# The final store split over two queues, and the instruction streams emitted into a Block, in a one-core decode kernel

## The chip, the cores and the metric

The kernel runs on one core of a Trainium2 chip. A core has five engines with instruction streams of their own: TensorE (PE, with its weight loads shown as PEld), VectorE (DVE), ScalarE (ACT), GpSimd (POOL) and SyncE (SP), and 16 DMA engines that carry the transfers which SP and ACT issue here. The engines are kept in step by semaphores alone. The metric is the device time of one execution in microseconds (us); less is better.

## The reference

One token is decoded. With `xn`, the normalised input, the output is `x + A(xn) + B(xn)`: A is attention with grouped heads over a long cache, B a small block that mixes shifted channels and then applies a two-layer MLP.

```python
# A: 32 query heads, 4 key/value heads, cache of 65536 positions, head size 128, D = 1024
q = (xn_A @ wq).reshape(1, 1, 32, 128).transpose(0, 2, 1, 3)
scores = einsum("bhqd,bhkd->bhqk", q, repeat(k_cache, 8, axis=1)) * 128 ** -0.5
o = einsum("bhqk,bhkd->bhqd", softmax(scores), repeat(v_cache, 8, axis=1))
A = o.transpose(0, 2, 1, 3).reshape(1, 1, 4096) @ wo
# B: F = 3584
h = gelu(layernorm(xn) @ w1)
x1 = xn + concat(shifted quarters of h) @ w2
B = x1 + gelu(layernorm(x1) @ w3) @ w4
return x + A + B          # 1 x 1 x 1024, bfloat16
```

The K and V caches are 67 MB each; with the weights, 170 MB are read from memory, and 2 KB are written.

## The kernel before

**Tiles.** K and V come in pairs of sub-tiles: a transfer of 4 MB brings 16384 positions of one head into one of two slots of `Kn` or `Vn`. Each sub-tile of 8192 positions (`NT` = 32 of them) goes through the same steps: VectorE transposes it (`Ttr`, line 463), TensorE multiplies with the queries (`QK`, line 475), VectorE and TensorE find a bound of the maximum (lines 482 to 492), ScalarE takes exponentials (`EXP`, line 505), TensorE and VectorE turn the result (lines 514 and 516), TensorE multiplies with V (`PV`, line 523), and ScalarE and GpSimd fold it into a running sum (`FLASH`, lines 531 to 537). The weights of B and of the output projection are loaded and used between sub-tiles, at places listed in `w_seq`. The last of them, w4, comes in four parts into the K slots (`w4_parts`), the smallest part last.

**Queues.** The order of each engine's work is written out by hand. An object of the class `_Q` (line 14) collects, for each engine, a list of waits, operations and transfers; `_op`, `_grp` and `_dma` (line 116) add to it, and work out from the buffers' last readers and writers which semaphores must be waited for. Only at the end does `emit` (line 43) go through a list and produce the engine's instructions. A wait that an instruction can't carry itself becomes a semaphore instruction with the line number 46. All loads are issued by SP, in the order of the list, but for the input `x` (2 KB), which ACT issues as its first instruction (line 275). The first loads are the two halves of wq (line 272), then K and V of the first pair (line 286).

**The opening.** What is built ahead of the kernel's function (line 640) fills a few constants on POOL and ends with a barrier over all five engines: four of them drain and count up one semaphore, POOL drains, waits for the four, and counts up a second semaphore, for which the four wait. After the barrier each engine's stream goes on with its own first instruction, without a jump.

**The end.** The output is summed in PSUM over all stages in four rows of 256 columns, on partitions 0, 32, 64 and 96 (`out_rows`, line 391). After the last part of w4 VectorE casts them into `orow` (line 618), SP issues one transfer of four rows of 512 bytes (line 619) and waits until it has landed. Then SP's stream is over; the other engines' streams end with their own last operation.

Of the kernel before, what the change touches and what calls it, by code (L numbers as in the profile page):

```python
# [72 lines left out]
def _deps(q, reads, writes):  # L73
    for b in reads:
        for s, v in b.w.items():
            q.wait((s, v))
    for b in writes:
        for s, v in b.w.items():
            q.wait((s, v))
        for s, v in b.r.items():  # L80
            q.wait((s, v))


def _done(ev, reads, writes, partial=False):
    for b in reads:
        b.add_read(ev)
    for b in writes:
        if partial:
            b.add_write(ev)
        else:  # L90
            b.set_write(ev)


def _op(q, fn, reads=(), writes=(), partial=False):
    _deps(q, reads, writes)
    ev = q.op(fn, True)
    _done(ev, reads, writes, partial)
    return ev
# [17 lines left out]
def _dma(q, chan, fn, reads=(), writes=(), partial=False):  # L116
    _deps(q, reads, writes)
    chan.n += 1
    ev = q.dma(fn, chan.sem, 16 * chan.n)
    _done(ev, reads, writes, partial)  # L120
    return ev


def bass_parallel_sum__gqa_block_cached__mixer_s_mlp__decode_kernel(
# [29 lines left out]

    with ExitStack() as es:
        E = es.enter_context

        def sb(name, shape, dt):
            return E(nc.sbuf_tensor(name, shape, dt))

        def ps(name, shape, dt):
            return E(nc.psum_tensor(name, shape, dt))

        def sem(name):
            return E(nc.semaphore(name))

# [51 lines left out]
        orow = sb("orow", [P, 256], BF)  # L218
# [15 lines left out]
        q_pe = _Q("pe", sem("c_pe"))  # L234
        q_dve = _Q("dve", sem("c_dve"))
        q_act = _Q("act", sem("c_act"))
        q_pool = _Q("pool", sem("c_pool"))
        q_sp = _Q("sp", None)
        chans = {}

        def chan(name):
            if name not in chans:
                chans[name] = _DmaChan(sem("d_" + name))
            return chans[name]
# [83 lines left out]
        def layer_norm(src, b_src, dst_f, dst_bf, b_dst, c0):  # L328
# [29 lines left out]
            reads=[b_M1, b_misc], writes=[b_misc])  # L358
# [19 lines left out]
        for h in range(HKV):  # L378
            for we in range(4):
# [3 lines left out]
                    reads=[b_M1, b_const], writes=[b_Y], partial=(h + we > 0))  # L383
# [232 lines left out]
        for i in range(len(w4_parts)):  # L616
            w4_pe(i)
        _op(q_dve, lambda e: e.tensor_copy(orow[:, :], OUT_ps[:, 0:256]), reads=[b_OUT], writes=[b_orow])
        ev_out = _dma(q_sp, chan("out"), lambda e: e.dma_start(out=out[0, 0, :].rearrange("(j n) -> j n", j=4), in_=orow[0:97:32, :]), reads=[b_orow])
        q_sp.wait(ev_out)  # L620

        q_sp.emit(nc.sync)
        q_act.emit(nc.scalar)
        q_pool.emit(nc.gpsimd)
        q_dve.emit(nc.vector)
        q_pe.emit(nc.tensor)


# [26 lines left out]
```

## Time and profile before

| | us |
|---|---|
| median of 3 runs (402.83 to 402.92) | 402.84 |
| the profiled execution | 402.83 |
| its span, first to last instruction | 401.6 |

| engine | busy us | share of the span |
|---|---|---|
| DVE | 227.8 | 57% |
| PE | 187.7 | 47% |
| POOL | 62.0 | 15% |
| ACT | 48.4 | 12% |

The DMA engines read 169.87 MB, 423 GB/s over the span. The profile is taken on one execution; the span runs from the first instruction of the program to the last, and the time of the execution is 1.23 us longer. In the views that follow, a line L272 is line 272 of the kernel before; SPq or POOLq is the sequencer of that engine, which issues transfers, waits and drains; an arrow `<-` in brackets names what ended the idle time ahead of a group. The chain of work that ended last is 54% DMA, 24% DVE and 17% PE.

### The profile page before, as it was taken

Reading aid. Unit: us, or ns where it says so; the run is one execution under the profiler, and the core shown is the slowest. Engines: PE = TensorE matmul, PEld = TensorE weight load, DVE = VectorE, ACT = ScalarE, POOL = GpSimd, SP = SyncE. Lnnn points to the kernel's source line nnn. Section 1 sums busy time; section 2 is a strip of 40 time slices with the busy share of each in tenths; the row PEclk is TensorE's granted clock in tenths of the full one; section 3 lists DMA queues with packets and bytes.
Section 4 is the critical chain, followed back from the end, with each engine's and each line's share of the span. In section 5 each row is a group of like instructions: output and inputs, shape, how many; then the busy total and the mean of one; then the engine's idle time right before and its main releaser. Section 6 shows DMA issues by size and latency. Waiting matters only on the chain.

```text
span 401.6 us, 5142 instructions
## 1 busy us (share of the span) xinstructions
PE 187.7 (47%) x2043; PEld 84.2 (21%) x2059; DVE 227.8 (57%) x400; ACT 48.4 (12%) x127; POOL 62.0 (15%) x90
## 2 busy tenths in 40 slices
PE   0361445064525745275630966353433545344674
PEld 0250111021103511062110731121111311111142
DVE  0217666277806588255753387676836775778410
ACT  0000211011101011011110011111201111112100
POOL 5000013011211011110310102111110102122110
PEclk9999999999855565555565555665565855656556
DMA  8999999999999999999999999999999999999995
GB/s 353 431 416 433 447 421 419 447 436 421 441 441 420 419 441 437 424 434 436 428 426 444 436 421 428 442 434 427 424 450 418 439 441 424 421 428 431 437 420 217
DMA packets 7088, 170.20 MB, mean 424 GB/s; under 512 B 916, under 2 KB 920, under 8 KB 1048
## 3 DMA queue, kind: packets, MB, share of 16 engines
q1 hardware_dynamic: 6920, 169.87, 98.4%
q8 instruction: 16, 0.26, 0.2%
q14 instruction: 8, 0.07, 0.0%
q10 hardware_dynamic: 144, 0.00, 0.0%
HBM read 169.87 MB, written 0.00 MB: 423 GB/s over the span
## 4 chain that ended last, share of the span: by engine, by line
DMA 54%; DVE 24%; PE 17%; issue 2%; ACT 2%; another core or an unknown queue 1%; SPq 0%; POOL 0%; ACTq 0%
DMA Kn<-in_A_k_cache_dram 43%; DVE X L463 12%; DMA Kn<-in_B_w_dram 6%; DMA Vn<-in_A_wq_dram 5%; PE H_ps L366 4%; DVE pT_f L516 3%; PE S_ps L475 3%; PE OT_ps L523 3%; DVE mrow L482 3%; PE M_ps L366 2%; ACT p_sb L505 2%; PE PT_ps L514 1%; PE M_ps L551 1%; PE OUT_ps L391 1%; DVE Yall L380 1%
## 5 line engine op out<-in xcount | busy, mean ns | idle before, releaser
L463 DVE STREAM_TRANSPOSE X<-Kn 128x1024 f32<-128x1024 f32 x128 | 151.7, 1215 | 64.5 <-DMA Kn<-in_A_k_cache_dram 64.5
L523 PE MATMUL OT_ps<-Vn,pT_f 128*32 128x512 bf16 x512 | 59.9, 620 | 54.1 <-DVE pT_f L516 54.1
L475 PE MATMUL S_ps<-X,Yall 128*32 128x512 bf16 x512 | 58.0, 598 | 17.0 <-DVE X L463 17.0
L488 PE MATMUL MB_ps<-Rm,Lmat 128*128 128x16 bf16 x32 | 6.2, 193 | 87.7 <-DVE Rm L483 87.7
L537 POOL TENSOR_TENSOR O_acc<-O_acc,tmpO 128x513 f32<-128x513 f32 x28 | 32.9, 1176 | 89.1 <-ACT tmpO L531 89.1
L535 POOL TENSOR_SCALAR O_acc<-O_acc,ff 128x513 f32<-128x513 f32 x28 | 19.6, 700 | 150.7 <-ACT ff L510 150.7
L505 ACT ACTIVATE p_sb<-S_ps,brun 128x512 bf16<-128x512 f32 x32 | 22.0, 688 | 173.1 <-DVE brun L503 154.6
L482 DVE TENSOR_REDUCE mrow<-S_ps 128x1 f32<-128x512 f32 x32 | 21.6, 674 | 24.6 <-PE S_ps L475 24.6
L531 ACT ACTIVATE tmpO<-OT_ps 128x512 f32<-128x512 f32 x32 | 19.2, 598 | 107.8 <-PE OT_ps L523 107.8
L475 PEld LDWEIGHTS S_ps<-X,Yall 128*32 128x32 bf16 x512 | 16.5, 126 | 54.7 <-DVE X L463 38.6
L516 DVE STREAM_TRANSPOSE pT_f<-PT_ps 128x512 f32<-128x512 f32 x32 | 22.9, 716 | 7.8 <-PE PT_ps L514 4.2
L523 PEld LDWEIGHTS OT_ps<-Vn,pT_f 128*32 128x32 bf16 x512 | 14.6, 128 | 59.4 <-DVE pT_f L516 42.7
L488 PEld LDWEIGHTS MB_ps<-Rm,Lmat 128*128 128x128 bf16 x32 | 3.3, 103 | 112.2 <-DVE Rm L483 112.2
L514 PE MATMUL PT_ps<-p_sb,permR 128*128 128x512 bf16 x16 | 9.5, 594 | 21.2 <-ACT p_sb L505 21.2
L366 PEld LDWEIGHTS H_ps<-xn_bf,W 128*128 128x128 bf16 x224 | 14.4, 172 | 1.7 <-issue 1.7
L366 PE MATMUL H_ps<-xn_bf,W 128*128 128x1 bf16 x224 | 14.5, 202 | 0.0
L514 PEld LDWEIGHTS PT_ps<-p_sb,permR 128*128 128x128 bf16 x32 | 3.4, 106 | 42.4 <-ACT p_sb L505 42.4
L492 DVE TENSOR_REDUCE Bst<-MB_ps 128x1 f32<-128x16 f32 x32 | 5.6, 174 | 8.3 <-PE MB_ps L488 8.3
L330 PE MATMUL M_ps<-ln_s,ones_f 128*128 128x1 f32 x6 | 1.8, 362 | 17.5 <-DVE ln_s L329 17.5
L533 POOL COPY O_acc<-tmpO 128x513 f32<-128x513 f32 x4 | 2.5, 615 | 47.5 <-ACT tmpO L531 47.5
L551 PE MATMUL M_ps<-O_acc,cb_W 128*128 128x128 f32 x32 | 7.4, 403 | 2.0 <-DVE cb_W L544 2.0
L391 PE MATMUL OUT_ps<-Kn,gh_bf 128*1 128x256 bf16 x112 | 5.8, 370 | 3.5 <-DMA Kn<-in_B_w_dram 3.5
(101 smaller groups left out, 114.0 us busy)
## 6 DMA issues: line engine op xcount, KB each, us to landing
Kn<-in_A_k_cache_dram SPq DMA_DIRECT2D x15, 4096.0 KB, 27.4
Vn<-in_A_v_cache_dram SPq DMA_DIRECT2D x15, 4096.0 KB, 22.3
W<-in_B_w_dram SPq DMA_DIRECT2D x2, 3584.0 KB, 25.1
W<-in_A_wo_dram SPq DMA_DIRECT2D x3, 2048.0 KB, 23.2
Kn<-in_A_wq_dram SPq DMA_DIRECT2D x1, 4096.0 KB, 12.3
Vn<-in_A_wq_dram SPq DMA_DIRECT2D x1, 4096.0 KB, 21.4
W<-in_B_w_dram SPq DMA_DIRECT2D x2, 2048.0 KB, 32.2
Kn<-in_A_k_cache_dram SPq DMA_DIRECT2D x2, 2048.0 KB, 24.8
```

The costliest lines, as they stand in the source:

```text
L366: fns.append(lambda e, j=j, cx=cx: e.matmul(ps_tile[:, c0 + cx:c0 + cx + 1], lhs_fn(j - j0, cx), rhs_fn(j), start=(j == 0 and cx == 0), st ...
L463: _op(q_dve, lambda e, ix=ix: e.transpose(out=X32[:, xs, 1024 * ix:1024 * (ix + 1)], in_=Kn32[:, s, 4096 * half + 1024 * ix:4096 * half + ...
L475: fns.append(lambda e, we=we, cm=cm, mv=mv: e.matmul(S_ps[32 * cm:32 * cm + 32, :], Yall[:, h, we, :, :].rearrange("p a g -> p (a g)"), mv ...
L482: _op(q_dve, lambda e: e.reduce_max(mrow[:, m:m + 1], S_ps[:, :], axis=AX.X), reads=[b_S], writes=[b_mrow[m]])
L505: _op(q_act, lambda e: e.activation(p_sb[:, m, :], S_ps[:, :], ACTF.Exp, bias=brun[:, kn:kn + 1], scale=SCALE, accum_out=tmpO[:, m, 512:513]),
L514: _op(q_pe, lambda e: e.matmul(PT_ps[:, :], permR[:, :], p_sb[:, m, :], start=True, stop=True), reads=[b_p[m], b_const], writes=[b_PT])
L516: _op(q_dve, lambda e: e.transpose(out=pT_f[:, :], in_=PT_ps[:, :]), reads=[b_PT], writes=[b_pT])
L523: fns.append(lambda e, q=q, q4=q4: e.matmul(OT_ps[32 * q4:32 * q4 + 32, :], pT_bf[:, q, :, 1], Vn[:, s, 8192 * half + 512 * q:8192 * half ...
L531: _op(q_act, lambda e: e.activation(tmpO[:, m, 0:512], OT_ps[:, :], ACTF.Copy), reads=[b_OT], writes=[b_tmpO[m]], partial=True)
L535: _op(q_pool, lambda e: e.tensor_scalar(out=O_acc[:, :], in0=O_acc[:, :], scalar1=ff[:, m:m + 1], scalar2=0.0, op0=ALU.mult, op1=ALU.add), ...
L537: _op(q_pool, lambda e: e.tensor_tensor(out=O_acc[:, :], in0=O_acc[:, :], in1=tmpO[:, m, :], op=ALU.add), reads=[b_tmpO[m]], writes=[b_Oacc])
L551: fns.append(lambda e, t=t: e.matmul(M0_ps[:, 128:256], cb_W[:, t, :, :].rearrange("p g i -> p (g i)"), O_acc[:, t * P:(t + 1) * P], start ...
```

## The change

The function opens a `Block`, and instead of emitting the five lists one after another into the program, it hands each to the block. In the built program each engine then has a part of its own: after the opening barrier it branches to this part, at the end of the part it branches to a common end part, and in the end part all five engines go through a barrier of the same build as the opening one. The store is two transfers, of two rows each, to the two halves of the output: SP issues rows 0 and 1, ACT issues rows 2 and 3, each as soon as `orow` is written. SP waits for both. The order of all other instructions on each engine is as before; line numbers after the edit are one higher, and after the store three higher.

```diff
     with ExitStack() as es:
         E = es.enter_context
+        block = E(nc.Block())
...
         _op(q_dve, lambda e: e.tensor_copy(orow[:, :], OUT_ps[:, 0:256]), reads=[b_OUT], writes=[b_orow])
-        ev_out = _dma(q_sp, chan("out"), lambda e: e.dma_start(out=out[0, 0, :].rearrange("(j n) -> j n", j=4), in_=orow[0:97:32, :]), reads=[b_orow])
-        q_sp.wait(ev_out)
-
-        q_sp.emit(nc.sync)
-        q_act.emit(nc.scalar)
-        q_pool.emit(nc.gpsimd)
-        q_dve.emit(nc.vector)
-        q_pe.emit(nc.tensor)
+        out_j = out[0, 0, :].rearrange("(j n) -> j n", j=4)
+        for q, j0 in ((q_sp, 0), (q_act, 2)):
+            ev_out = _dma(q, chan("out%d" % j0), lambda e, j0=j0: e.dma_start(out=out_j[j0:j0 + 2, :], in_=orow[32 * j0:32 * j0 + 33:32, :]), reads=[b_orow])
+            q_sp.wait(ev_out)
+
+        block.sync(lambda e: q_sp.emit(e))
+        block.tensor(lambda e: q_pe.emit(e))
+        block.vector(lambda e: q_dve.emit(e))
+        block.scalar(lambda e: q_act.emit(e))
+        block.gpsimd(lambda e: q_pool.emit(e))
```

## The prediction, made before the changed kernel was run

> **What bounds the kernel now.** I read the page's slices first, then the chain that ended last, then the two ends of the run, because the change touches only what comes before the first load and after the last sum. The slices and the span:
>
> ```profile
> span 401.6 us, 5142 instructions
> ...
> DMA  8999999999999999999999999999999999999995
> GB/s 353 431 416 433 447 421 419 447 436 421 441 441 420 419 441 437 424 434 436 428 426 444 436 421 428 442 434 427 424 450 418 439 441 424 421 428 431 437 420 217
> ```
>
> The transfer engines are full from the first slice to the last but one. The kernel is a stream of 170 MB, and its length does not depend on which engine is how busy: what starts the stream later moves the end by the same amount, and what is added behind its last byte is added to the time. The last part of the chain (start us, length us, what):
>
> ```profile
> 374.88 23.88 DMA Kn<-in_B_w_dram
> 398.76 0.04 issue
> 398.80 0.62 PE OUT_ps L391 x7
> 399.42 0.02 issue
> 399.45 0.42 DVE orow L618
> ```
>
> The last load of w4 is issued at 374.88 and lands 23.9 us later, a transfer of 512 KB that stands in line behind earlier ones; so some 15 us and more of queued work covers any small delay of the engines in the middle. Behind it come eight matmuls, the cast into `orow`, and the store:
>
> ```profile
> 399.90 0.65 SPq L619 DMA_DIRECT2D out_dram<-orow  x1
> ```
>
> ```profile
> SPq L46 <- PE OT_ps L523: 155.5, 14, 16.5
> SPq L46 <- DVE X L463: 122.2, 13, 20.9
> ...
> SPq L46 <- DMA out_dram<-orow: 1.0, 1, 1.0
> ```
>
> In these waits of SP (total us, times, longest) the last row is the wait for the store. In the trace's own events the store's issue begins at 399.899, its semaphore is complete at 401.558 (1.66 us), and SP's wait, the last instruction, ends at 401.59. That is the span; the profiled execution took 402.83, so 1.23 us lie outside it. The median of the runs is 402.84, so a sum made for this execution holds for the median to 0.01.
>
> The opening of the program has one barrier over five engines, of the same build as the one which the change adds at the end (ns least/median/most, first and last start in us):
>
> ```profile
> L640 POOLq EVENT_SEMAPHORE  x2: 17/17/17, 0.6 to 0.7; - x2
> ...
> L640 POOLq DRAIN  x1: 173/173/173, 0.4 to 0.4; - x1
> ...
> L640 SPq EVENT_SEMAPHORE  x1: 17/17/17, 0.7 to 0.7; - x1
> ...
> L640 PEldq EVENT_SEMAPHORE  x1: 51/51/51, 0.7 to 0.7; - x1
> ```
>
> ```profile
> 0.79 0.39 SPq L272 DMA_DIRECT2D Kn<-in_A_wq_dram  x1
> 0.80 0.40 ACTq L275 DMA_DIRECT2D x_bf<-in_A_x_dram  x1
> ```
>
> **The change, part by part.** The program's order shows what each engine gains: one branch between the opening barrier and its first instruction, one branch after its last, and in an end part one drain and one semaphore wait (POOL a drain and two). SP also gains one wait; the store of four rows becomes one of two rows on SP and one of two rows on ACT. No arithmetic is removed.
>
> *SP's first branch.* It stands in front of the load at 0.79, with nothing beside it, so it moves the whole stream. No row shows a branch. Below, it costs one step of the sequencer: SP's barrier wait ends at 0.726 and its load begins at 0.791, 0.07. Above, it costs a gap in which an engine has instructions to run but none at hand: TensorE shows one in this run, 1.55 us from the matmul that starts at 25.03 to the weight load that starts at 26.585.
>
> ```profile
> 22.74 2.45 PE L366 MATMUL M_ps<-xn_bf,Vn 128*128 128x1 bf16 x86 [0.46 <-DMA Vn<-in_A_wq_dram]
> 26.59 1.28 PE L366 MATMUL M_ps<-xn_bf,Vn 128*128 128x1 bf16 x42 [1.39 <-issue]
> ```
>
> Nearest in kind, I judge, is the POOL drain of 0.173, after which POOL's next instruction takes 0.044 to begin (0.545 to 0.589): like a branch, it lets nothing behind it start. I take **0.22**.
>
> The Trainium skill (Advanced Engine Details and Errata, Control Flow Timing) gives about 51 ns for a branch that is always taken. No row here shows one; with 0.05 at both of SP's branches the sum below would be 0.56 and the time 403.39.
>
> *The first branches of the others, 0.* ACT's delays the load of x by 0.22. The first user waits for it:
>
> ```profile
> 13.26 0.17 DVE L326 CAST xT<-x_bf 128x8 f32<-128x8 bf16 x1 [11.80 <-DMA x_bf<-in_A_x_dram]
> ```
>
> The layer norm and the first half of the projection follow, and then TensorE sits idle 0.46 us for the second half of wq (the bracket at 22.74 above): this covers 0.22. If x came later than that, the K load at 22.38, which waits for TensorE's first half, would go out later, with 8 MB (K and V of the first pair, some 20 us at 424 GB/s) still in line: nothing at the end either. POOL's constants are ready at 6.3 and first used at 13.68; DVE's one early operation ends at 1.46 and its next is at 13.26; TensorE starts at 13.68.
>
> *The store.* The data is 2 KB: four packets of about 25 ns between 401.15 and 401.24. Its 1.66 us are 0.65 of issue, 0.6 until the packets and 0.3 until the semaphore, and two shorter rows keep all of these. Bounds: a gain of 0.32 if the issue fell to the shortest load issue (0.33), a loss of 0.65 if the second store's issue waited for the first's. The nearest row is the opening, where SP and ACT issue side by side, 0.393 from 0.791 and 0.404 from 0.796: no waiting, and ACT ends 0.02 later. I take **+0.02**. On ACT only its end branch stands behind the store, and ACT has been idle since about 380. SP's extra wait for the second semaphore is one step, **0.07** (0.03 to 0.10).
>
> *SP's last branch*, bounds as for the first: **0.22**, bare, since SP is the last to arrive. The other engines' last branches lie beside the store: TensorE is done at 399.42, DVE at 399.88, ACT at about 400.55, POOL at 379.4, all over 1 us before 401.56. Without that cover each would cost what SP's costs.
>
> *The end barrier.* SP's drain takes 0.01, waking POOL 0.01 to 0.02; from POOL's first wait (0.589) to the moment TensorE has passed the barrier (0.784) it is 0.195: **0.21** (0.15 to 0.30).
>
> *Outside the span.* After the last instruction the trace still shows one semaphore being counted up by the engines in turn. Now four of its five steps come early (399.585 to 400.021) and only SP's is late (401.708); with the barrier all five are late. Four steps of the way back (401.708 to 401.870) take 0.16: **+0.16**, from 0 if they proceed side by side to 0.44 (the four early ones, DVE's lateness included).
>
> *Sum:* 0.22 + 0.02 + 0.07 + 0.22 + 0.21 + 0.16 = 0.90. 402.83 + 0.90 = 403.73, and 403.74 beside the median. The low ends add up to 0.07 − 0.32 + 0.03 + 0.07 + 0.15 + 0 = 0.00 (402.84), the high ends to 1.55 + 0.65 + 0.10 + 1.55 + 0.30 + 0.44 = 4.59 (407.4).
>
> **The rivals.**
>
> *Cheap branches.* If a branch is one step of 0.07, the sum is 0.90 − 0.30 = 0.60 and the time 403.44. For it: register and semaphore instructions of the sequencers take 17 to 51 ns here. Against it: a branch has to redirect the stream of instructions, which none of those does.
>
> *An instruction gap at SP's branch.* If one of SP's two branches has to wait for instructions as TensorE did, that one costs 1.55: 0.90 + 1.33 = 2.23, time 405.07; both, 406.4. For it: nothing on SP covers such a gap. Against it: the target of each branch is, in SP's own stream, the very next instruction, and SP's stream is short (88 instructions, 92 after).
>
> The Trainium skill (Runtime: NRT & Kernel Launch, Instruction fetch mechanics) says that a taken branch to a target outside the two pages held must wait for a page to be transferred. The trace fits the mechanism on TensorE: a 16 KB packet of its instruction queue starts at 24.23, just ahead of the gap. By that rule a target close by costs no such wait, and the sum stays at 0.90.
>
> *The store gets shorter with its rows.* The place is the stretch from 399.90 to 401.56. If its 1.66 us went with the rows per queue, two rows would take 0.83, and the sum would be 0.07: 402.91, not slower. It decides from a saving of 0.09 on, where the total falls under the bound of 0.2% given next. For it: the store's issue is the longest of all (0.65 against 0.33 to 0.43), with the fewest rows. Against it: just that; a load of 128 rows issues faster, so rows do not set the length.
>
> **How the numbers follow.** A measurement of this kernel can tell about 0.2%, 0.81 us, from no change: within it is 402.03 to 403.65. Chances: forecast 0.55 (403.74, its own range 403.5 to 404.4), cheap branches 0.25, an instruction gap 0.13, a shorter store 0.07. Slower: 0.48 of the forecast's 0.55 (the rest lies under 403.65) and the 0.13 make 0.61. Within: 0.07 + 0.25 + 0.03 of the store's = 0.35. Faster by over 0.2% needs the halved store and cheap branches and steps at once: 0.04. The range 403.1 to 405.1 leaves out the shorter store (0.07), two gaps or a longer one (0.06) and the low tail of cheap branches (0.03).
>
> **What would show it.** The first load should begin near 1.0 instead of 0.79 and the last matmul and the cast should move by as much; both stores should begin within 0.02 of each other and land about 1.66 us later; the span should end about 0.5 us after the landing instead of 0.03, with the rest of the time outside growing by 0.16. The prediction is wrong if the stream itself gets longer or shorter by more than its start moves, if a gap of over 1 us stands before SP's first load or after its last wait, or if the two stores land far apart.

## The result

The changed kernel takes 404.09 us (median of 6 runs, 404.02 to 404.29), the kernel before, in the runs beside it, 402.85 (402.69 to 402.98). The ratio is 1.0032, with a 95% interval of 1.0019 to 1.0045: slower, by 1.24 us. The forecast was 403.74 with a range of 403.1 to 405.1; its sum of added costs was 0.90.

The page of the changed kernel: the span, and the same two rows of 40 slices.

```profile
span 402.4 us, 5155 instructions
...
DMA  8999999999999999999999999999999999999994
GB/s 358 424 415 445 433 420 435 443 422 427 450 427 419 445 420 435 432 443 425 431 434 433 427 435 437 422 433 442 414 440 443 428 430 430 422 429 433 448 409 183
```

The stream of loads is as full as before. The span is 0.8 longer, but the time is 1.24 longer: part of the loss lies outside the span, in the closing of the program.

The opening, from the view in order of time (start us, length us, engine, line, operation):

```profile
0.79 0.39 SPq L273 DMA_DIRECT2D Kn<-in_A_wq_dram  x1
0.80 0.41 ACTq L276 DMA_DIRECT2D x_bf<-in_A_x_dram  x1
```

The first load still starts at 0.79 (0.793; before 0.791; in the kernels without a Block it lies between 0.791 and 0.796). The branch in front of it costs nothing. The end of the chain that ended last (start us, length us, what), and the stores in order of time:

```profile
375.52 23.36 DMA Kn<-in_B_w_dram
398.88 0.04 issue
398.93 0.62 PE OUT_ps L392 x8
399.55 0.02 issue
399.58 0.42 DVE orow L619
```

```profile
400.03 0.63 SPq L622 DMA_DIRECT2D out_dram<-orow  x1
400.03 1.34 ACTq L622 DMA_DIRECT2D out_dram<-orow  x1
```

The cast starts 0.13 later than in the profiled execution of before. Both stores begin together, but ACT's issue takes 1.34 us where SP's takes 0.63. What SP waited for (total us, times, longest), and the instructions of the Block's end part (ns least/median/most, first and last start in us):

```profile
SPq L46 <- DMA out_dram<-orow: 1.2, 1, 1.2
...
SPq L155 <- PEq L155: 0.2, 1, 0.2
```

```profile
L155 POOLq EVENT_SEMAPHORE  x2: 17/17/17, 402.2 to 402.3; - x2
L155 POOLq DRAIN  x1: 1204/1204/1204, 382.5 to 382.5; - x1
L155 PEldq DRAIN  x1: 640/640/640, 398.9 to 398.9; - x1
L155 DVEq DRAIN  x1: 464/464/464, 399.6 to 399.6; - x1
L155 ACTq DRAIN  x1: 153/153/153, 401.4 to 401.4; - x1
L155 SPq COMPARE_BRANCH  x1: 33/33/33, 402.0 to 402.0; - x1
L155 SPq DRAIN  x1: 13/13/13, 402.1 to 402.1; - x1
...
L155 PEldq EVENT_SEMAPHORE  x1: 51/51/51, 402.3 to 402.3; - x1
```

Of the ten branches in the built program this is the only one in the trace: the one on SP that carries a wait. That wait is for SP's own half, which had landed at 401.63, before the branch began at 401.97; so the time that the branch takes is not waiting. The four other engines' drains lie ahead of it and cost nothing, POOL's 1.2 us included, because they begin early. After the store's landing there remain SP's branch, its drain, and the barrier, which is the 0.2 in the last row of SP's waits.

From the traces' own events, in us, the two profiled executions (402.83 and 404.09) divide as follows:

| stretch | before | after | difference |
|---|---|---|---|
| up to the first store's issue | 399.899 | 400.028 | +0.13 |
| from there to the last landing | 1.659 | 1.866 | +0.21 |
| from the last landing to the end of the span | 0.033 | 0.462 | +0.43 |
| outside the span | 1.24 | 1.73 | +0.49 |
| sum | 402.83 | 404.09 | +1.26 |

Two questions were open: why ACT's half lands late, and why the part outside the span grows by 0.49 where 0.16 was expected.

### The profile page after: what moved, and what is told of

Its sections match the earlier page's. It is cut to its first block, busy times and chain, and to the rows that moved or that the text cites. A ratio compares the mean times of both kernels' runs of the same rounds, so it can differ in the third digit from the quotient of the medians.

```text
span 402.4 us, 5155 instructions
## 1 busy us (share of the span) xinstructions
PE 185.8 (46%) x2043; PEld 82.9 (21%) x2059; DVE 227.7 (57%) x400; ACT 48.3 (12%) x127; POOL 61.8 (15%) x90
## 4 chain that ended last, share of the span: by engine, by line
DMA 54%; DVE 24%; PE 17%; issue 2%; ACT 1%; another core or an unknown queue 1%; SPq 0%; POOL 0%; ACTq 0%
DMA Kn<-in_A_k_cache_dram 43%; DVE X L464 13%; DMA Kn<-in_B_w_dram 6%; DMA Vn<-in_A_wq_dram 5%; PE H_ps L367 4%; PE S_ps L476 3%; DVE pT_f L517 3%; PE OT_ps L524 3%; DVE mrow L483 3%; PE M_ps L367 2%; ACT p_sb L506 1%; PE PT_ps L515 1%; PE M_ps L552 1%; PE OUT_ps L392 1%; DVE Yall L381 1%
```

## The experiments

The diffs stand against the changed kernel for the first two, and against the kernel of before for the rest, where nothing else is said. Each kernel's median stands beside that of the kernel before on the same chip. The columns after the ratio are from its own profiled execution: from the first store's issue to the last landing, from there to the end of the span, and the part outside the span.

| kernel | median us (before) | ratio, 95% interval | issue to landing | to the end | outside |
|---|---|---|---|---|---|
| Block, old store | 403.77 (402.89) | 1.0022 [1.0013, 1.0031] | 1.68 | 0.40 | 1.72 |
| split store, no Block | 403.05 (402.89) | 1.0003 [0.9994, 1.0011] | 1.86 | 0.05 | 1.24 |
| all engines wait | 403.49 (402.89) | 1.0014 [1.0005, 1.0023] | 1.68 | 0.08 | 1.74 |
| whole store from ACT | 402.93 (402.89) | 1.0001 [0.9992, 1.0010] | 1.67 | 0.03 | 1.25 |
| POOL waits | 403.47 (402.91) | 1.0015 [1.0006, 1.0025] | 1.67 | 0.04 | 1.77 |
| ACT, DVE, PE wait | 403.23 (402.91) | 1.0007 [0.9998, 1.0016] | 1.68 | 0.08 | 1.51 |
| half a store, from ACT | 402.79 (402.91) | 0.9997 [0.9988, 1.0007] | 1.61 | 0.03 | 1.24 |
| Block, drain behind the store | 403.64 (402.91) | 1.0018 [1.0009, 1.0027] | 1.66 | 0.30 | 1.72 |
| halves in series on SP | 404.35 (402.86) | 1.0035 [1.0021, 1.0049] | 3.11 | 0.03 | 1.23 |
| halves back to back on SP | 403.42 (402.92) | 1.0011 [1.0002, 1.0020] | 2.17 | 0.05 | 1.25 |
| the changed kernel again | 403.90 (402.86) | 1.0027 [1.0016, 1.0037] | 1.87 | 0.45 | 1.74 |

**The Block with the old store.**

```diff
-        out_j = ...
-        for q, j0 in ((q_sp, 0), (q_act, 2)):
-            ev_out = _dma(q, chan("out%d" % j0), ...)
-            q_sp.wait(ev_out)
+        ev_out = _dma(q_sp, chan("out"), lambda e: e.dma_start(out=out[0, 0, :].rearrange("(j n) -> j n", j=4), in_=orow[0:97:32, :]), reads=[b_orow])
+        q_sp.wait(ev_out)
```

> The Block with the old store (four rows, SP). Theory: of the +1.26 us between the two profiled executions, 0.21 are the ACT store that lands late (1.87 us from issue to landing in place of 1.66), 0.13 are the load stream's own wobble, and the rest, about 0.9, is the Block: 0.4 between the landing and the end of the span (branch, drain, barrier) and 0.5 outside it. So 403.7 to 403.8, with 1.66 us for the store and about 1.7 us outside the span. Rival, the split costs nothing and the Block all: 404.0 to 404.1.

403.77: the Block costs 0.88 of the 1.24, and the rival (all of it) falls. In the profiled execution it is 0.37 between landing and end and 0.49 outside the span.

**The split store without the Block.**

```diff
-        block = E(nc.Block())
...
-        block.sync(lambda e: q_sp.emit(e))
+        q_sp.emit(nc.sync)
...
```

> The split store without the Block. Theory: ACT's issue takes 1.3 us again because it overlaps SP's, its half lands 0.2 to 0.3 us later than the store of before, the span grows by that and the part outside stays at 1.23: 403.05 to 403.15. Rival, the long ACT issue was chance and the split is free: 402.85, with an ACT issue of 0.65. Third, two halves are quicker: below 402.7.

The store's issues in this kernel, from the view of their line (ns):

```profile
L621 SPq DMA_DIRECT2D out_dram<-orow x1: 629/629/629, 399.9 to 399.9; - x1
L621 ACTq DMA_DIRECT2D out_dram<-orow x1: 1337/1337/1337, 399.9 to 399.9; - x1
```

ACT's long issue is not chance: it is 1.34 in all three runs with the split on two queues. SP's half lands after 1.60, ACT's after 1.86, and the part outside stays at 1.24. The median is 0.16 up, inside the interval of no change; the 0.2 is read from the trace, not from the times.

**All engines wait for the store, no Block.**

```diff
         q_sp.wait(ev_out)
+        for q in (q_act, q_pool, q_dve, q_pe):
+            q.wait(ev_out)
```

> The kernel of before, with a wait for the store at the end of each of the four other engines' streams: no Block, no branch, no barrier. Theory: the 0.5 us outside the span come from all five engines reaching the closing round of the program late, so they come here too: span 401.6, outside 1.65 to 1.75, time 403.25 to 403.35. Rival, they come from the Block's own end part (its drains and its barrier, or the fetching of instructions behind the branch): outside stays at 1.23, time 402.85.

With no branch, drain or barrier added, the part outside the span is 1.74, as with the Block, and the median grows by 0.60 (403.49, which is 0.14 over the range expected, though the part outside is as forecast). So the 0.49 are not the Block's own instructions. They come from engines that end late. In the view of the waits' line the last wait of each engine is at the end of the span:

```profile
L46 PEldq EVENT_SEMAPHORE  x141: 51/51/2180, 6.3 to 401.7; - x141
L46 ACTq EVENT_SEMAPHORE  x65: 17/17/13582, 43.8 to 401.7; - x65
L46 POOLq EVENT_SEMAPHORE  x61: 17/17/43, 6.3 to 401.7; - x61
L46 DVEq EVENT_SEMAPHORE  x56: 21/21/21, 13.6 to 401.7; - x56
L46 SPq EVENT_SEMAPHORE  x37: 17/28/28, 22.2 to 401.7; - x37
```

**POOL alone waits; the three others wait.** Which late engine it is, the counts of the closing semaphore tell. Once their streams are over, the engines count it up nine times in a first round, in a fixed order, each count waiting for the one ahead of it. (A second round of nine follows; the way to it takes 0.78 to 0.79 in every kernel, so the differences lie in the first.) These are the first five counts (us behind the end of the span; a negative number is ahead of it):

```
                 1      2      3      4      5
before        -2.01  -1.97  -1.93  -1.57   0.12
after          0.24   0.27   0.49   0.53   0.55
all wait       0.19   0.23   0.50   0.54   0.57
POOL waits    -2.02  -1.99   0.54   0.58   0.60
three wait     0.19   0.23   0.26   0.31   0.33
```

Count 3 seemed to be POOL's, and to come 0.54 to 0.57 after POOL's last instruction, so two kernels split the four waits.

```diff
         q_sp.wait(ev_out)
+        q_pool.wait(ev_out)
```

> The kernel of before, with a wait for the store at the end of POOL's stream alone. Theory: in the closing round after the span, POOL takes about 0.55 us from its last instruction to its own count (0.54 to 0.57 in the three runs in which all engines end late), SP only 0.12, and the counts that follow POOL's wait for it; so POOL alone gives nearly the whole of the part outside: 1.65 to 1.72, time 403.3 to 403.4. Rival, each late engine adds a step of about 0.1: outside 1.3 to 1.4, time 402.95 to 403.05.

```diff
         q_sp.wait(ev_out)
+        for q in (q_act, q_dve, q_pe):
+            q.wait(ev_out)
```

> The kernel of before, with the wait for the store at the end of ACT's, DVE's and PE's streams, not POOL's. Theory: ACT takes 0.27 us to its count (seen where ACT issues the store), then three steps of 0.04, 0.04 and 0.02 and a turn of 0.10 follow, in place of SP's 0.12 and 0.04: outside 1.24 + 0.27 = 1.51, time 403.15 to 403.25, less than with all four. Rival, each late engine adds a step: with three of four engines 1.55 to 1.65.

```profile
L46 ACTq EVENT_SEMAPHORE  x64: 17/17/13508, 44.2 to 378.1; - x64
L46 POOLq EVENT_SEMAPHORE  x61: 17/17/43, 6.3 to 401.6; - x61
```

These are the same rows in the kernel in which POOL alone waits: ACT's last wait is back at 378.1, and still the part outside is 1.77, even a little over the 1.65 to 1.72 expected. (The median, 403.47, is also 0.07 over.) The rows of the other kernel, in which POOL's last wait is early:

```profile
L46 ACTq EVENT_SEMAPHORE  x65: 17/17/13490, 44.2 to 401.6; - x65
L46 POOLq EVENT_SEMAPHORE  x60: 17/17/43, 6.3 to 379.0; - x60
```

Without POOL's lateness the part outside is 1.51, as expected. (This is read from the trace; the interval of its median includes no change.) So lateness does not add up by engine: the slowest way into the closing round decides, and that is POOL's.

**The whole store from ACT; half a store from ACT.**

```diff
-        ev_out = _dma(q_sp, chan("out"), ...)
+        ev_out = _dma(q_act, chan("out"), ...)
```

> The kernel of before, with the whole store (four rows) issued by ACT in place of SP. Theory, ACT's issue is long only where it overlaps SP's: issue 0.65, landing after 1.66, time 402.85. Rival, a store from ACT is slow by itself: issue near 1.3, landing 0.2 to 0.7 later than SP's, time 403.05 to 403.5.

The second, against the split store without the Block, leaves rows 0 and 1 of the output unwritten:

```diff
-        for q, j0 in ((q_sp, 0), (q_act, 2)):
+        for q, j0 in ((q_act, 2),):
```

> No Block; rows 2 and 3 alone are stored, by ACT, and rows 0 and 1 of the output are not written. Theory: the late landing of ACT's half comes from the two stores being issued at the same moment; alone it lands 1.60 to 1.67 us after its issue begins, with an issue of 1.05 to 1.1 as in the four-row store from ACT. Rival, two rows from ACT are slow by themselves: 1.86, with an issue of 1.33.

The line of the store in the first and in the second of these:

```profile
L619 ACTq DMA_DIRECT2D out_dram<-orow x1: 1092/1092/1092, 399.9 to 399.9; - x1
```

```profile
L621 ACTq DMA_DIRECT2D out_dram<-orow x1: 1079/1079/1079, 399.8 to 399.8; - x1
```

Both theories of the first were half wrong: ACT's issue is long by itself, 1.09 against SP's 0.65, and yet the store lands after 1.67, as SP's does. Between two engines, the length of an issue does not tell when the data lands. Two rows alone, from ACT, land after 1.61. So neither ACT nor the two rows make the half late; what is left, and what differs between this kernel and the split one, is SP's store issued at the same time. The packets say where the time goes. Here are 1.5 us from 400.5 on in 40 slices, first of the split store without the Block (both issues begin at 399.9), then of the half store from ACT (399.8):

```profile
GB/s 0 0 0 0 0 0 0 0 0 0 0 0 0 0 0 0 14 14 0 0 0 0 0 0 27 0 0 0 0 0 0 0 0 0 0 0 0 0 0 0
GB/s 0 0 0 0 0 0 0 0 0 0 0 0 0 0 14 14 0 0 0 0 0 0 0 0 0 0 0 0 0 0 0 0 0 0 0 0 0 0 0 0
```

In the first row SP's half moves first and ACT's second. From the traces' own events, ACT's packets begin 1.24 after the start of its issue when it is alone and 1.50 when SP issues too, while SP's begin after 1.23 with ACT's beside them and without. The delay lies ahead of the first packet, not in moving 1 KB. On ACT it goes with the issue: that grows by 0.26 as well (1.08 to 1.34), and the first packet follows its end by 0.16 both times.

**A drain that carries the wait,** against the Block with the old store.

```diff
-        block.sync(lambda e: q_sp.emit(e))
+        block.sync(lambda e: (q_sp.emit(e), e.drain()))
```

> The Block with the old store, and one more instruction on SP at the end of its part, a drain, which carries the wait for the store in place of the branch. Theory: a branch that carries no wait leaves nothing in the program that runs (none of the nine others shows in the trace), and the branch with the wait costs 0.17 us; a drain costs 0.06 to 0.08. So the stretch from landing to the end of the span falls from 0.40 to 0.29 to 0.32, time 403.65 to 403.7. Rival, the branch is there all the same and the drain comes on top: 0.45 to 0.50, 403.85.

SP's branch and drain in the end part, with the old store, first with the branch that waits and then with the added drain (on its own line, 623) in its place:

```profile
L155 SPq COMPARE_BRANCH  x1: 33/33/33, 401.7 to 401.7; - x1
L155 SPq DRAIN  x1: 13/13/13, 401.9 to 401.9; - x1
```

```profile
L155 SPq DRAIN  x1: 7/7/7, 401.8 to 401.8; - x1
```

The branch is gone from the trace, and landing to end falls from 0.40 to 0.30. (The medians, 403.77 and 403.64, do not by themselves tell the two kernels apart.) A branch without a wait costs nothing here; one with a wait takes 0.17 from its start to the next instruction. Why a branch without a wait leaves nothing, no run here shows.

**Both halves on SP.** In the first of these kernels SP's wait for the first half stands between the two issues (against the split store without the Block):

```diff
-        for q, j0 in ((q_sp, 0), (q_act, 2)):
+        for q, j0 in ((q_sp, 0), (q_sp, 2)):
```

> No Block; both halves of the store issued by SP, one after the other. Theory: what makes ACT's half late is the overlap of two issues, not the split; on one queue the second issue begins when the first is over, 0.66 to 0.70 us later, and its half lands 1.60 us after that: 2.27 from the start of the first, the span grows by about 0.65, the outside stays at 1.24, time 403.45 to 403.6. Rival, the two are pipelined behind the first issue: 2.0 or less, 403.25.

So it measures two stores in series (1.60 and 1.50); its 404.35 is over both expectations, and it tells neither theory from the other. It does show SP's half alone: 1.60, as beside ACT's. The second kernel issues both and waits afterwards:

```diff
-        ev_out = _dma(q_sp, chan("out"), ...)
-        q_sp.wait(ev_out)
+        out_j = ...
+        evs = [_dma(q_sp, chan("out%d" % j0), ...) for j0 in (0, 2)]
+        for ev_out in evs:
+            q_sp.wait(ev_out)
```

> No Block; both halves issued by SP back to back, and SP waits for both only after the second issue (the kernel with both halves on SP had its wait between the two). Theory: the second issue begins when the first is over, 0.65 to 0.70 us after the first began, and lands 1.5 to 1.6 after its own start, so the last landing is 2.15 to 2.3 after the first issue's start, in place of 1.66 for one store and 1.86 for two queues; span 402.1 to 402.25, outside 1.24, time 403.4 to 403.5. Rival: what a store waits for is shared by both, and the second lands 1.86 to 2.0 after the first's start, as with two queues: 403.05 to 403.2.

```profile
L620 SPq DMA_DIRECT2D out_dram<-orow x2: 488/559/630, 400.2 to 400.9; - x2
```

The second issue waits for the first, and the last landing comes after 2.17. Two queues (1.86) do save issue time against one queue; they do not reach one transfer (1.66).

**The changed kernel again.**

> The changed kernel once more, beside the same runs of before as the two-halves kernel. Theory: the parts add up, 0.37 from the Block inside the span, 0.49 outside it, 0.21 from the late half and 0.06 from SP's second wait, 1.13 in all: 403.95 to 404.1, and the stretch from issue to landing is 1.85 to 1.88 again. Rival, there is a part not yet found, some 0.1 to 0.15 in the load stream: 1.24 or more, with the cast ending at about 400.0 while it ends at 399.87 in the kernel of before of the same chip.

403.90, 1.04 over its companions, a little under the 1.13 that the parts add up to and under the range expected; the store takes 1.87 again, and the cast ends at 399.96. The rival, a hidden part in the load stream, needed 1.24 or more. Over the four kernels with a Block the medians differ from their parts by +0.11, +0.01, −0.02 and −0.09, so no such part is left. Among the kernels without a Block the end of the cast ranges from 399.78 to 400.15; the 0.13 between the two first profiles is within that scatter.

No kernel that writes the whole output beats the one before; the whole store from ACT equals it.

## Why the prediction was right, and where its terms were off

The direction and the size to within 0.35 us held, and most of the mechanism: the stream is untouched, the loss stands behind the last byte, and it is made of the barrier, SP's last branch, the late closing and the store. But one term of the sum, SP's first branch, has no counterpart, and that the sum came so near is in part luck: the terms taken too high (0.30 together) and those taken too low (0.66 with the scatter) offset each other. The terms, with what the first pair of profiles shows:

| term | taken | measured |
|---|---|---|
| SP's first branch | 0.22 | 0.00 |
| the store | 0.02 | 0.21 |
| SP's second wait | 0.07 | 0.04 |
| SP's last branch | 0.22 | 0.17 |
| end barrier, SP's drain included | 0.21 | 0.22 |
| outside the span | 0.16 | 0.49 |
| scatter of the load stream | 0 | 0.13 |

(The measured values of the third to fifth row are the steps from landing to branch, branch to drain, and drain to end, 0.07, 0.17 and 0.22, the first of them less the 0.03 that the old wait took. The column adds up to the 1.26 between the two profiled executions.)

*SP's first branch* was the step that failed outright: it lies below its own lower bound of 0.07. Nine of the ten branches leave neither a record nor a gap; the drain kernel shows the tenth vanish too once its wait is moved. So the argument from the order of the built program was not enough; the 0.22 taken from POOL's drain was a fair price for the branch that does show, at 0.17.

The Trainium skill's price for an always-taken branch (Advanced Engine Details and Errata, Control Flow Timing: about 51 ns) is not tested by the bare ones, which leave nothing in the trace, and is under the 0.17 that the one with a wait takes, from its start to the next instruction. That one appears in the trace under the name of a compare-and-branch, for which the same section gives about 108 ns; the measured 0.17 is over this too.

*The store* was mis-sized, about in the middle of its bounds of −0.32 and 0.65. The nearest row, the opening, where SP and ACT issue side by side without loss, did not carry over: SP's store delays ACT's half by 0.26 (SP's own half is not delayed), of which 0.05 is won back because a half lands sooner than the whole.

*Outside the span* was mis-sized, and just above its upper bound of 0.44. The mechanism was right, the counting round that waits for late engines, and all-engines-wait shows it without a Block. But the step priced four hops at the pace at which they follow each other; the cost is one engine's own way into the round, POOL's 0.54 to 0.57. Of the 0.49, the fifth count is 0.44 later, and the step behind it takes 0.10 in place of 0.04.

The other branches, constants and the load of x cost nothing, as argued.

The rivals: the cheap branches were right at the start and not at the end. Over both, the 0.17 measured is nearer to this rival's 0.14 than to the 0.44 of the forecast; what carried the time into the forecast's own range, and past the rival's 403.44, are the 0.52 by which the store and the closing exceed their terms. No gap for instructions showed at any branch of SP. A two-row store does land sooner, by 0.05, not by half.

Of the signs named in advance, the stores that begin together, the span that ends about 0.5 behind the landing and the absence of a gap of over 1 us came true. The first load at 1.0 did not, nor the growth of only 0.16 outside. The two halves landed 0.27 apart (401.63 and 401.89), which the prediction had put, without a size, among the signs of being wrong; for the store it was wrong.

Some readings in the prediction are a little off, without weight for the sum: 402.83 less 401.59 is 1.24, not 1.23; one load's issue took 0.56 (the first of V), outside the 0.33 to 0.43 given for loads; and POOL's last operation ends at 383.7, not 379.4, ACT's at 382.5.

What stays open: what SP's and ACT's issues share, and why POOL's way into the closing round is the longest. The two issues were not tried with a stagger between them, nor on two queues with other sizes.

## What to carry to other kernels

A barrier at the end of a program can cost more than its instructions. Here the barrier took 0.22 us, but it made engines that had finished long before finish last, and the closing of the program, which waits for the slowest of them, took 0.49 more. Let idle engines' streams simply end, and let the one engine that must wait for the last store be the only late one. The store of 2 KB took 1.66 us, of which its packets took 0.08: splitting it over two queues had 0.05 to win and lost 0.21.

## What the runs showed of the hardware

- From the last instruction of an engine to its count in the closing round: SP 0.12, ACT 0.27, POOL 0.54 to 0.57 us.
- A branch that carries a wait took 0.16 to 0.17 us even where the wait was already met; the nine without one left no record and no gap.
- ACT takes 1.08 to 1.09 us to issue a store that SP issues in 0.63 to 0.66, and both land after 1.6 to 1.7; beside SP's, ACT's issue takes 1.34. For the loads at the opening the two take the same, 0.39 and 0.40.
- SP's issue of the third part of w4 took 0.43 in the profile of before and 1.08 in the changed kernel's. It is not the change: over the thirteen profiles, with and without a Block, four show 0.43 and nine 0.77 to 1.31. Nor does the end follow it: the cast ends at 399.87 with 1.31 and at 400.03 with 0.43.
